# Attention followed by top-1 expert routing: earlier weight loads, shorter routing bookkeeping, and the left-over tile moved to the end

## The chip, the cores and the metric

The kernel runs on one core of a Trainium2 chip. A core has a matrix engine (TensorE, PE in the profile), a vector engine (VectorE, DVE), an engine for activations (ScalarE, ACT), a general engine (GpSimd, POOL), an engine that here only starts transfers (SyncE, SP) and 16 DMA engines that all transfers share. Each compute engine works through its own list of instructions in order and waits for the others at semaphores. The metric is the device time of one execution in microseconds (us). The kernel before was run three times: 325.83, 327.12 and 322.86 us, median 325.83. The profile is of a further execution of 325.04 us, whose span from the first to the last instruction is 323.0 us.

## The reference, cut to what matters

```python
kv  = einsum('bhsd,bhse->bhde', k, v)              # b=8, h=8, s=576, d=64
o   = einsum('bhsd,bhde->bhse', q, kv)             # attention without softmax
x   = o / sqrt(mean(o*o) + 1e-6) * g_norm          # per head; then 4608 rows x 512
logits = x @ w_gate                                # 8 experts
expert = argmax(logits);  gate = softmax(logits)[expert]
for e in range(8):                                 # w1: 512 x 1024, w2: 1024 x 512
    xe = x[expert == e]
    out[expert == e] = gate * (relu(xe @ w1[e]) @ w2[e])
```

Inputs and outputs are in 32-bit floats. Every row goes to exactly one expert; how many rows an expert gets is known only at run time.

## The kernel before, in words

**Attention stage (up to about 135 us).** The 4608 rows are treated in 36 *slots* of 128 rows. Four groups P of two batches each have nine slots: four for the first batch, four for the second, and one for the remaining 64 + 64 rows. For a batch, k-transposed-times-v is summed in PSUM (`kv_mm`), copied out, and extended with gate columns (`kv_gate`), so that the product with q gives the output rows and the logits at once. A slot s consists of `x_qt` (transposes of q, two slots ahead), `x_qs` (ScalarE copies them out), `x_mm` (the product, tile `op`), and `x_norm` with its inner `rest` (the norm: ScalarE squares `op` into `sq`, VectorE sums to `ms`, ScalarE makes `lnt` and `rinv`, VectorE writes `lr`, the scaled logits, and `xg`, the scaled rows in 16 bits).

Rows of `xg` are 516 sixteen-bit values wide: 512 of data, then the row's token number (512:514) and its gate weight (514:516).

**Routing.** Every four or five slots (a `Route`) the rows so far are sorted. `first` makes the one-hot choice `oh`; `ranks` counts, with matmuls of ones and of a triangular matrix, how many earlier rows chose the same expert (tile `pp`); `send` turns this into a row number `sli` in the DRAM scratch `xs_scratch`, which has 4608 places for each expert (`eoff` holds 4608 x e); `scatter` lets GpSimd start an indirect DMA of 128 rows to their places. A running count per expert (`csum`) carries over from group to group.

**Order.** All five engines' lists are written by hand: the loop over the 36 slots calls what the lists `mid[s]`, `late[s]` and `last[s]` hold, filled by `at(...)` (lines 440 to 487). `mid` runs before the slot's norm, `late` between `ms` and `lr`, `last` at the end of the slot. `pace` puts a tiny GpSimd copy ahead of each scatter, which reads `lr` of a named slot and so holds the scatter back until that slot. Loads of q, k and v (tag `ld`, six buffers of 8 KB per partition) and of expert weights are issued by SyncE in program order; each waits for its buffer to be free.

**Seam.** After slot 35 the last two tiles are routed (`tail`), the final counts become `cnt`, `valid`, `bigm` and the table of rows to gather, `rowi`. Expert 0's weights were loaded during slot 21's place in the order; ScalarE now casts them to 16 bits (`half1` also multiplies w1 by the norm's gain, `half2` casts w2). Expert 1's two loads are issued here, w1 when expert 0's w1 is cast, w2 when its w2 is cast, because one 32-bit staging buffer serves each. Then GpSimd gathers rows of experts 0 and 1 from `xs_scratch` (lines 609 and 719). A gather can start only when all scatters have landed. While it waits, TensorE runs `zeros` (matmuls of zeros that keep it busy, line 126).

**Expert stage.** Every expert has five tiles of 128 rows; rows beyond 640 of an expert go to left-over tiles. In this draw there is one. A `Job` has `flip(t)` (turn a tile: four transposes, a VectorE copy into `xt`, and the output row numbers `idx`), `one(ws, f)` (four matmuls of 320 columns, tile `hp`, then Relu on ScalarE into `ht`; sixteen of these), and `two(t)` (eight matmuls of 512 columns, tile `yp`, the gate weight on VectorE into `ys`, and a scatter to the output). In the loop over jobs (line 729) the next expert's weights are cast between the matmuls: `half1` on VectorE beside `one`, `half2` on ScalarE beside `two`, and as each staging buffer falls free the load of the expert after next is issued. The turns of the next expert's tiles stand among the last `one`s. The order of the jobs is experts 0 to 6, then the left-over tile, then expert 7. The left-over tile's expert number is read from a table at run time, so its loads are addressed by a register. If there were more left-over tiles, a loop after expert 7 (line 759) would take them.

The two pools of tiles, one for attention and one for the experts, use the same memory one after the other.

Of the kernel before, what the change touches and what calls it, by code (L numbers as in the profile page):

```python
# [11 lines left out]
F32 = mybir.dt.float32  # L12
F16 = mybir.dt.float16
# [15 lines left out]
def kernel(  # L29
# [11 lines left out]
    nc = tc.nc  # L41
# [41 lines left out]
    c_f32 = nc.inline_tensor(c32, name="c_f32")  # L83
    c16 = np.zeros((128, 384), np.float16)
    c16[:, 0:128] = np.eye(128)
    c16[:, 128:256] = ar[:, None] < ar[None, :]
    c16[:, 256:384] = 1.0
    c_f16 = nc.inline_tensor(c16, name="c_f16")

# [3 lines left out]
    cf = P_const.tile([128, c32.shape[1]], F32, tag="cf")  # L93
    ch = P_const.tile([128, 384], F16, tag="ch")
    ident = cf[:, 0:128]
# [7 lines left out]
    utri = ch[:, 128:256]  # L103
    ones = ch[:, 256:384]
    wg = P_const.tile([128, 4, 8], F32, tag="wg")
    g2 = P_const.tile([128, 1], F32, tag="g2")
    gw = P_const.tile([128, 4, 2, 8], F32, tag="gw")
    epsb = P_const.tile([128, 1], F32, tag="epsb")
    csum = P_const.tile([128, 8], F32, tag="csum")
    valid = P_const.tile([128, E, CT], F32, tag="valid")  # L110
# [18 lines left out]
    class Weights:  # L129
        def __init__(self, e):  # L130
            self.e = e if isinstance(e, bass.DynSlice) else slice(e, e + 1)

        def stage1(self):
            self.s1 = P_w.tile([128, 4, F], F32, tag="ws1", bufs=1, name="ws1")
            nc.sync.dma_start(
                self.s1, moe_w1[self.e, :, :].rearrange("o (t p) f -> p (o t) f", p=128)
            )

        def stage2(self):
            self.s2 = P_w.tile([128, 8, D], F32, tag="ws2", bufs=1, name="ws2")  # L140
            nc.sync.dma_start(
                self.s2, moe_w2[self.e, :, :].rearrange("o (t p) d -> p (o t) d", p=128)
            )

        def half1(self, eng, kk):
            if kk == 0:
                self.w1 = P_w.tile([128, 4, F], F16, tag="w1e", bufs=2, name="w1e")
            if eng is nc.scalar:
                eng.activation(self.w1[:, kk, :], self.s1[:, kk, :], ACTF.Copy, scale=g2)
            else:  # L150
                eng.tensor_scalar(  # L151
                    self.w1[:, kk, :], self.s1[:, kk, :], g2, 1.0,
                    op0=ALU.mult, op1=ALU.mult,
                )

        def half2(self, kk):
            if kk == 0:
                self.w2 = P_w.tile([128, 8, D], F16, tag="w2e", bufs=2, name="w2e")
            nc.scalar.copy(  # L159
                self.w2[:, 2 * kk:2 * kk + 2, :], self.s2[:, 2 * kk:2 * kk + 2, :]  # L160
            )

    ENG = mybir.EngineType
    by_hand = {ENG.PE, ENG.Activation, ENG.DVE, ENG.Pool, ENG.SP}
    order = list(range(E - 1)) + ["left", E - 1]
    W = [Weights(e) if e != "left" else None for e in order]

    with (
# [119 lines left out]
        qts, xgs, lrs = {}, {}, {}  # L288
        tail = None

        def x_qt(s):
# [32 lines left out]
        def x_norm(s, op):  # L324
            P, r, b = split(s)
            if r == 0:
                xgs[P] = PA.tile([128, 9, RW], F16, tag="xg", bufs=2, name="xg")
                lrs[P] = PA.tile([128, 9, 8, 8], F32, tag="lr", bufs=2, name="lr")
            xg, lr = xgs[P], lrs[P]
            oc = op[:, :, 0:288].rearrange("p c (i n) -> p c i n", n=144)  # L330
# [29 lines left out]
        class Route:  # L360
# [3 lines left out]
            def first(self):  # L364
# [19 lines left out]
                nc.vector.tensor_tensor(self.oh, cd, _bc(m2, 2, 8), op=ALU.is_equal)  # L384
                self.cs16 = PA.tile([128, 8], F16, tag="cs16", bufs=2, name="cs16")
                nc.vector.tensor_copy(self.cs16, csum)
                self.dl = dl

            def ranks(self):

                G, oh = self.G, self.oh
                self.pp = PSA.tile([128, G, 8], F32, tag="misc", bufs=1, name="pp")
                pp = self.pp
                nc.tensor.matmul(pp, ones, _bc(self.cs16, 1, G), start=True, stop=False)
                for t in range(G - 1):
                    nc.tensor.matmul(
                        pp[:, t + 1:G, :], ones, _bc(oh[:, t, :], 1, G - 1 - t),
                        start=False, stop=False,
                    )
                nc.tensor.matmul(pp, utri, oh, start=False, stop=True)  # L400
                ex = PA.tile([128, G, 8], F32, tag="ex", bufs=2, name="ex")
                nc.scalar.activation(ex, self.dl, ACTF.Exp)
                tsum = PA.tile([128, 8], F32, tag="tsum", bufs=2, name="tsum")
                nc.vector.reduce_sum(tsum, oh.transpose([0, 2, 1]), axis=AXX)
                nc.vector.tensor_add(csum, csum, tsum)
                se = PA.tile([128, G], F32, tag="se", bufs=2, name="se")
                nc.vector.reduce_sum(se, ex, axis=AXX)
                xg, g0 = xgs[self.P], self.g0
                nc.vector.reciprocal(
                    xg[:, g0:g0 + G, 514:516].bitcast(F32).rearrange("p g o -> p (g o)"), se  # L410
                )
                nc.vector.tensor_copy(
                    xg[:, g0:g0 + G, 512:514].bitcast(I32).rearrange("p g o -> p (g o)"),
                    tokc[:, 9 * self.P + g0:9 * self.P + g0 + G],
                )

            def send(self):
                G, g0 = self.G, self.g0
                t1 = PA.tile([128, G, 8], F32, tag="t1", bufs=2, name="t1")
                nc.vector.tensor_tensor(t1, self.pp, _bc(eoff, 1, G), op=ALU.add)  # L420
                t2 = PA.tile([128, G, 8], F32, tag="t2", bufs=2, name="t2")
                nc.vector.tensor_tensor(t2, t1, self.oh, op=ALU.mult)
                sl = PA.tile([128, G], F32, tag="sl", bufs=2, name="sl")
                nc.vector.reduce_sum(sl, t2, axis=AXX)
                sli = PA.tile([128, G], I32, tag="sli", bufs=4, name="sli")
                nc.vector.tensor_copy(sli, sl)
                self.sli = sli

# [46 lines left out]
        for P, g0, G in groups + [(3, 0, 4), (3, 4, 3)]:  # L475
            rt = Route(P, g0, G)
            s = 9 * P + g0 + G - 1
            at(last, s, rt.first)
            at(mid, s + 2, rt.ranks)
            at(late, s + 2, rt.send)  # L480
            s0 = s + 2 if P == 3 or (P, g0) == (2, 4) else s + 3
            for t in range(G):
                at(last, min(s0 + t, 35), pace, min(s0 + t, 35))
                at(last, min(s0 + t, 35), rt.scatter, t)

        at(last, 21, W[0].stage1)
        at(last, 21, W[0].stage2)


        load_first()  # L490
        nc.vector.memset(zero16, 0.0)
        nc.vector.memset(epsb, 1e-6)
        nc.vector.memset(csum, 0.0)
        nc.vector.memset(gw, 0.0)
# [45 lines left out]
        tail.ranks()  # L540
        cs16 = PA.tile([128, 8], F16, tag="cs16", bufs=2, name="cs16")
        nc.vector.tensor_copy(cs16, csum)
        tail.send()
        for t in range(2):
            tail.scatter(t)
        cp = PSA.tile([128, 8], F32, tag="misc", bufs=1, name="cp")
        nc.tensor.matmul(cp, ones, cs16, start=True, stop=True)
        nc.vector.tensor_copy(cnt, cp)
        nc.vector.tensor_tensor(valid, _bc(rankc, 1, E), _bc(cnt, 2, CT), op=ALU.is_lt)
# [4 lines left out]
        for kk in range(4):  # L554
            W[0].half1(nc.scalar, kk)
        W[1].stage1()
        for kk in range(4):
            W[0].half2(kk)
        W[1].stage2()


    with (
# [142 lines left out]
        with tc.manual_schedule(engines=by_hand):  # L705
# [17 lines left out]
            zp = PSF.tile([128, 512], F32, tag="yp", bufs=3, name="yp")  # L723
            zeros(zp, 8)
            for t in range(3):
                jobs[0].flip(t)
                zeros(zp, 2)

            for n in range(len(order)):
                job = jobs[n]  # L730
                if n == 3:
                    jobs[7] = left_over(0, 3 * CT, out_views[E * CT])
                    W[7] = jobs[7].w
                nxt = jobs[n + 1] if n + 1 < len(order) else None
                rows(n + 2)
                flips = list(range(nxt.nt)) if nxt is not None else []
                for ws in range(job.halves):
                    for f in range(8):
# [3 lines left out]
                        if ws == job.halves - 1 and f >= 2 and flips:  # L742
                            nxt.flip(flips.pop(0))
                        if ws == 0 and f % 2 == 1 and nxt is not None:
                            W[n + 1].half1(nc.vector, f // 2)
                            if f == 7 and n + 2 < len(order):
                                W[n + 2].stage1()
                for kk in range(max(job.nt, 4)):
                    if kk < job.nt:
                        job.two(kk)  # L750
                    if kk < 4 and nxt is not None:
                        W[n + 1].half2(kk)
                        if kk == 3 and n + 2 < len(order):
                            W[n + 2].stage2()
# [44 lines left out]
```

## Time and profile before

| What | Value | From |
|---|---|---|
| span of the profiled execution | 323.0 us | head of the page |
| TensorE busy | 275.5 us, 85% | page, part 1 |
| VectorE, ScalarE, GpSimd busy | 170.9, 158.1, 154.9 us | page, part 1 |
| bytes moved by DMA | 85.66 MB, mean 265 GB/s | page, part 2 |
| mean granted TensorE clock | 0.944 of full | the cores' view |
| last attention product starts (slot 35) | 129.65 us | timeline |
| first gather starts | 150.10 us | timeline |
| first expert matmul | 159.21 us | timeline |
| expert 1, start to end of its matmuls | 179.11 to 197.55 us | chain in order of time |
| left-over tile | 288.71 to 294.46 us | timeline |
| last expert's second products end | 317.74 us | timeline |

How to read it: the busy share of an engine is an average over three stages that are limited by different things, so it decides nothing by itself. One asks of each stage what the last wait before its end was. The timeline lists instructions by start; an entry such as `[3.95 <-ACT ht L663]` says that the engine stood idle for 3.95 us before it, and that the last thing to come was the ScalarE instruction of line 663 writing `ht`. A DMA instruction's row shows only its issue; its landing comes later. Numbers after an L are lines of the kernel before.

### The profile page before, as it was taken

How to read it: one execution, taken by the hardware profiler on the slowest of the kernel's cores; microseconds unless marked ns; L12 is line 12 of the kernel's file. 1: busy time of each engine (PE TensorE's matmuls, PEld its weight loads, DVE VectorE, ACT ScalarE, POOL GpSimd, SP SyncE). 2: the span in 40 equal slices, each digit the busy share in tenths (PEclk: the TensorE clock that was granted, in tenths of full speed). 3: DMA queues.
4: the chain of work that ended last, by engine and by line, in shares of the span. 5: the costliest groups of instructions: out<-in, count | busy, mean ns of one | idle time of the engine just before them, and what ended most of it. 6: DMA issues, size and time to landing. Idle time of an engine off the chain costs nothing.

```text
span 323.0 us, 6221 instructions
## 1 busy us (share of the span) xinstructions
PE 275.5 (85%) x2333; PEld 190.0 (59%) x2333; DVE 170.9 (53%) x467; ACT 158.1 (49%) x338; POOL 154.9 (48%) x208
## 2 busy tenths in 40 slices
PE   8787899999799976340799999999999999996893
PEld 3466788878687865210474655657475665654551
DVE  0042677787878778820266946455354546155022
ACT  1052455546456465380165573736466473834620
POOL 9322044448437654563773476467473315551014
PEclk9997999999999999565599999999999999999798
DMA  7999999999999950159457999979998978995004
GB/s 199 340 280 254 279 280 342 301 311 364 268 270 374 404 205 33 65 189 403 137 161 279 315 345 311 386 224 371 297 374 301 329 288 256 402 293 224 0 0 155
DMA packets 59759, 85.66 MB, mean 265 GB/s; under 512 B 16461, under 2 KB 41294, under 8 KB 59728
## 3 DMA queue, kind: packets, MB, share of 16 engines
q1 hardware_dynamic: 50480, 65.09, 63.9%
q0 software_dynamic: 6976, 18.96, 16.4%
q10 hardware_dynamic: 2272, 1.20, 1.4%
q8 instruction: 19, 0.31, 0.4%
q14 instruction: 12, 0.10, 0.1%
HBM read 71.70 MB, written 15.50 MB: 270 GB/s over the span
## 4 chain that ended last, share of the span: by engine, by line
PE 38%; DMA 11%; issue 4%; POOL 2%; DVE 1%; POOLq 1%
PE hp L656 18%; PE yp L670 16%; DMA out_dram<-ys,idx 10%; PE xp L637 3%; DMA xe<-xs_scratch,rowi 2%; POOL xs_scratch L430 1%; PE yp L126 1%; POOL out_dram L678 1%; DVE w1e L151 0%; POOLq L794 0%; POOL xe L609 0%; DVE xt L640 0%; POOLq L678 0%; POOLq L609 0%; DVE idx L642 0%
## 5 line engine op out<-in xcount | busy, mean ns | idle before, releaser
L663 ACT ACTIVATE ht<-hp 128x320 f16<-128x320 f32 (+1 forms) x136 | 57.7, 428 | 74.8 <-PE hp L656 50.1
L656 PE MATMUL hp<-xt,w1e 128*128 128x320 f16 (+1 forms) x544 | 81.6, 300 | 4.0 <-ACT ht L663 3.9
L678 POOL DMA_INDIRECT out_dram<-ys,idx x41 | 42.6, 1039 | 72.4 <-DVE ys L675 66.0
L670 PE MATMUL yp<-w2e,ht 128*128 128x512 f16 x328 | 72.3, 379 | 0.0
L656 PEld LDWEIGHTS <-w1e 128*128 128x128 f16 x544 | 51.6, 100 | 24.6 <-issue 4.7
L675 DVE TENSOR_SCALAR ys<-yp,xe 128x512 f32<-128x512 f32 x41 | 30.6, 750 | 58.0 <-PE yp L670 57.9
L670 PEld LDWEIGHTS <-ht 128*128 128x128 f16 x328 | 32.1, 98 | 37.1
L318 PE MATMUL op<-kvs,qts 128*128 128x144 f32 (+1 forms) x320 | 46.1, 307 | 8.5 <-DVE xg L353 4.1
L609 POOL DMA_INDIRECT xe<-xs_scratch,rowi x40 | 41.5, 1037 | 18.5 <-issue 14.3
L318 PEld LDWEIGHTS op<-kvs,qts 128*128 128x128 f32 (+1 forms) x320 | 38.4, 186 | 12.3 <-ACT sq L334 4.4
L430 POOL DMA_INDIRECT xs_scratch<-xg,sli x36 | 35.2, 978 | 12.9 <-issue 12.6
L640 DVE COPY xt<-xp 128x512 f16<-128x512 f16 x41 | 17.3, 423 | 39.9 <-PE xp L637 23.6
L159 ACT CAST w2e<-ws 128x1024 f16<-128x1024 f32 x36 | 34.8, 1042 | 2.7 <-DMA ws<-in_moe_w_dram 2.7
L236 POOL COPY qp<-ld 128x512 f32<-128x512 f32 x32 | 18.5, 615 | 31.8 <-DMA ld<-in_q_dram 31.8
L339 DVE TENSOR_REDUCE ms<-sq 128x8 f32<-128x512 f32 x36 | 24.4, 677 | 8.4 <-ACT sq L334 8.4
L637 PE MATMUL xp<-ch,xe 128*128 128x128 f16 x164 | 16.5, 226 | 13.5 <-DMA xe<-xs_scratch,rowi 12.7
L343 ACT ACTIVATE lnt<-ms,epsb 128x8 f32<-128x8 f32 x36 | 10.9, 302 | 34.3 <-DVE ms L339 34.3
L334 ACT ACTIVATE sq<-op 128x512 f32<-128x512 f32 x36 | 21.3, 590 | 10.9 <-PE op L318 10.6
L255 PE MATMUL kvp<-ld 128*64 128x64 f32 x512 | 21.9, 228 | 4.3 <-DMA ld<-in_v_dram 4.3
L353 DVE TENSOR_TENSOR xg<-op,rinv 128x512 f16<-128x512 f32 x36 | 24.5, 680 | 0.3 <-DMA xs_scratch<-xg,sli 0.3
L305 ACT COPY qts<-qtp 128x512 f32<-128x512 f32 x36 | 20.9, 581 | 6.5 <-PE qtp L300 6.4
L637 PEld LDWEIGHTS <-xe 128*128 128x128 f16 x164 | 12.9, 101 | 18.2 <-DMA xe<-xs_scratch,rowi 13.6
(92 smaller groups left out, 260.3 us busy)
## 6 DMA issues: line engine op xcount, KB each, us to landing
ws<-in_moe_w_dram SPq DMA_DIRECT2D x18, 2048.0 KB, 11.1
ld<-in_q_dram SPq DMA_DIRECT2D x8, 1024.0 KB, 10.7
ld<-in_k_dram SPq DMA_DIRECT2D x7, 1024.0 KB, 10.3
ld<-in_v_dram SPq DMA_DIRECT2D x7, 1024.0 KB, 10.6
kr<-in_k_dram SPq DMA_DIRECT2D x8, 128.0 KB, 9.9
ld<-in_k_dram SPq DMA_DIRECT2D x2, 512.0 KB, 7.3
ld<-in_v_dram ACTq DMA_DIRECT2D x2, 512.0 KB, 8.7
qr<-in_q_dram SPq DMA_DIRECT2D x8, 128.0 KB, 8.6
```

What stands on the lines that cost most here:

```text
L159: nc.scalar.copy(self.w2[:, 2 * kk:2 * kk + 2, :], self.s2[:, 2 * kk:2 * kk + 2, :])
L318: nc.tensor.matmul(op[c, i // 2, c0:c0 + 144], qts[s][:, i, c], kvs[:, i, :], start=True, stop=True,)
L339: nc.vector.reduce_sum(ms, sq, axis=AXX)
L353: nc.vector.tensor_tensor(xg[:, r, 0:512].rearrange("p (c i h n) -> p c i h n", c=2, i=2, h=2), ox, _bc(r4, 4, 64), op=ALU.mult,)
L430: nc.gpsimd.indirect_dma_start(out=xs_views[9 * self.P + self.g0 + t], out_offset=IndirectOffsetOnAxis(ap=self.sli[:, t:t + 1], axis=0), i ...
L609: nc.gpsimd.indirect_dma_start(out=xe.bitcast(I32), out_offset=None, in_=xs.ap(), in_offset=IndirectOffsetOnAxis(ap=rows, axis=0), bounds_ ...
L637: nc.tensor.transpose(xp[:, c, :], xe[t][:, c * 128:(c + 1) * 128], ident16)
L656: nc.tensor.matmul(hp, self.w.w1[:, kk, f * 128:(f + 1) * 128], self.xt[:, kk, ws * wd:(ws + 1) * wd], start=(kk == 0), stop=(kk == 3),)
L663: nc.scalar.activation(self.ht[:, f, ws * wd:(ws + 1) * wd], hp, ACTF.Relu)
L670: nc.tensor.matmul(yp, self.ht[:, f, t * 128:(t + 1) * 128], self.w.w2[:, f, :], start=(f == 0), stop=(f == 7),)
L675: nc.vector.tensor_scalar(ys, yp, self.xe[t][:, 514:516].bitcast(F32), None, op0=ALU.mult)
L678: nc.gpsimd.indirect_dma_start(out=self.views[t], out_offset=IndirectOffsetOnAxis(ap=self.idx[:, t:t + 1], axis=0), in_=ys, in_offset=None ...
```

## The change

It has six parts.

1. *Routing with fewer VectorE operations.* The running count starts from a constant that already holds each expert's offset (`base`, 36 x e in each of 128 partitions, so that the sum over partitions is 4608 x e). It is kept in 16 bits, a new tile for each group. So the copy of `csum` to 16 bits, the addition of `eoff` and the final cast of the index are no longer needed. The token numbers are written by GpSimd, once for nine slots. What `ranks` did on VectorE moves into `send`, behind the index.
2. *Scatters of the last group P = 3 without `pace`*, and two per slot.
3. *Expert 1's weights are loaded during attention*, into four buffers of the tag `ld` that q, k and v no longer use (`stage_in`), and are cast at the seam: w1 on VectorE, w2 on ScalarE in eight pieces of 512 columns.
4. *Expert 2's loads are issued early but held*: two one-element memsets on VectorE, behind the first three turns of expert 0, stand ahead of them.
5. *24 instead of 8 matmuls of zeros* at the seam.
6. *The left-over tile comes after expert 7.* The casts of the next expert's weights begin with job 1, as experts 0 and 1 have theirs.

```diff
-    c16 = np.zeros((128, 384), np.float16)
+    c16 = np.zeros((128, 392), np.float16)
...
+    c16[:, 384:392] = (N // 128) * np.arange(8)
...
+    base = ch[:, 384:392]
...
-        def stage1(self):
+        def stage1(self, hold=False):
             self.s1 = P_w.tile([128, 4, F], F32, tag="ws1", bufs=1, name="ws1")
+            if hold:
+                nc.vector.memset(self.s1[:, 0, 0:1], 0.0)
             nc.sync.dma_start(
...
+        def stage_in(self, pool, tag, bufs):
+
+            self.s1, self.s2 = [], []
+            for dst, src in ((self.s1, moe_w1), (self.s2, moe_w2)):
+                rows = src[self.e, :, :].rearrange("o (t p) f -> p (o t) f", p=128)
+                n = rows.shape[1] // 2
+                for m in range(2):
+                    t = pool.tile([128, n, rows.shape[2]], F32, tag=tag, bufs=bufs, name="ws")
+                    nc.sync.dma_start(t, rows[:, n * m:n * m + n, :])
+                    dst.extend([t[:, kk, :] for kk in range(n)])
...
+            if isinstance(self.s2, list):
+                for m in (2 * kk, 2 * kk + 1):
+                    nc.scalar.copy(self.w2[:, m, :], self.s2[m])
...
-    order = list(range(E - 1)) + ["left", E - 1]
+    order = list(range(E)) + ["left"]
...
+                nc.gpsimd.tensor_copy(
+                    xgs[P][:, :, 512:514].bitcast(I32).rearrange("p g o -> p (g o)"),
+                    tokc[:, 9 * P:9 * P + 9],
+                )
...
-                self.cs16 = PA.tile([128, 8], F16, tag="cs16", bufs=2, name="cs16")
-                nc.vector.tensor_copy(self.cs16, csum)
...
-                nc.tensor.matmul(pp, ones, _bc(self.cs16, 1, G), start=True, stop=False)
+                nc.tensor.matmul(pp, ones, _bc(csum[-1], 1, G), start=True, stop=False)
...
-                nc.vector.tensor_tensor(t1, self.pp, _bc(eoff, 1, G), op=ALU.add)
-                t2 = PA.tile([128, G, 8], F32, tag="t2", bufs=2, name="t2")
-                nc.vector.tensor_tensor(t2, t1, self.oh, op=ALU.mult)
...
+                nc.vector.tensor_tensor(t2, self.pp, oh, op=ALU.mult)
+                self.sli = PA.tile([128, G], I32, tag="sli", bufs=4, name="sli")
+                with nc.allow_low_precision("sums of whole numbers"):
+                    nc.vector.reduce_sum(self.sli, t2, axis=AXX)
...
+                with nc.allow_low_precision("sums of whole numbers below 2048"):
+                    nc.vector.reduce_sum(tsum, oh.transpose([0, 2, 1]), axis=AXX)
+                    nc.vector.tensor_add(cs, csum[-1], tsum)
+                csum.append(cs)
...
-                at(last, min(s0 + t, 35), pace, min(s0 + t, 35))
-                at(last, min(s0 + t, 35), rt.scatter, t)
+                if P < 3:
+                    at(last, s0 + t, pace, s0 + t)
+                at(last, min(s0 + t // (2 if P == 3 else 1), 35), rt.scatter, t)
 
         at(last, 21, W[0].stage1)
         at(last, 21, W[0].stage2)
+        at(last, 30, W[1].stage_in, PA, "ld", 6)
...
             W[0].half1(nc.scalar, kk)
-        W[1].stage1()
         for kk in range(4):
             W[0].half2(kk)
-        W[1].stage2()
+        for kk in range(4):
+            W[1].half1(nc.vector, kk)
+        for kk in range(4):
+            W[1].half2(kk)
...
-            zeros(zp, 8)
+            zeros(zp, 24)
             for t in range(3):
                 jobs[0].flip(t)
                 zeros(zp, 2)
 
+            W[2].stage1(hold=True)
+            W[2].stage2(hold=True)
...
-                if n == 3:
-                    jobs[7] = left_over(0, 3 * CT, out_views[E * CT])
-                    W[7] = jobs[7].w
+                if n == 4:
+                    jobs[E] = left_over(0, 3 * CT, out_views[E * CT])
+                    W[E] = jobs[E].w
...
-                        if ws == 0 and f % 2 == 1 and nxt is not None:
+                        if n > 0 and ws == 0 and f % 2 == 1 and nxt is not None:
...
-                    if kk < 4 and nxt is not None:
+                    if n > 0 and kk < 4 and nxt is not None:
```

## The prediction

> **What bounds the kernel now.** I read the busy slices of the page first. They put the lost time in two places.
>
> ```profile
> PE   8787899999799976340799999999999999996893
> ...
> PEclk9997999999999999565599999999999999999798
> DMA  7999999999999950159457999979998978995004
> ```
>
> Each digit is a slice of 8.07 us. TensorE drops from slice 14 to 19 (113 to 161 us), where the DMA engines stand nearly empty for two slices (15 and 16, up to 137 us) and then fill again. It drops once more near the end. The chain that ended last, in order of time, shows what the seam between attention and experts waits for:
>
> ```profile
> 142.48 0.96 POOL xs_scratch L430
> 143.44 5.68 issue
> ...
> 150.10 5.25 DMA xe<-xs_scratch,rowi
> ...
> 159.42 2.72 PE hp L656 x16
> ...
> 162.95 1.50 DVE w1e L151 x2
> ```
>
> The last scatter of rows starts at 142.48; the gathers, which must wait for all scatters, start only at 150.10 and the first lands 5.25 us later. The table by stretches says why both transfers are slow:
>
> ```profile
> 130.00:140.00 10.00, 3.36 (x27) 2.10 (x24) 8.24 (x42) 5.60 (x11) 6.04 (x12) 0.50 0.19 67
> 140.00:150.00 10.00, 2.70 (x7) 0.69 (x5) 0.00 (x0) 4.16 (x5) 2.84 (x3) 0.67 0.88 316
> 150.00:155.00 5.00, 0.00 (x0) 0.00 (x0) 0.00 (x0) 0.00 (x0) 3.98 (x4) 0.50 1.05 383
> ```
>
> The last three columns are clock, DMA share, GB/s. Expert 1's 4.2 MB go out at 140.41 and 144.19, just when scatters and gathers need the engines. The issue table for 121 to 140 us gives 2.5 us from issue to landing for a scatter with the engines free; over the whole run the median is 6.1.
>
> The timeline of the end shows the second loss:
>
> ```profile
> 295.94 3.88 ACT L159 CAST w2e<-ws 128x1024 f16<-128x1024 f32 x4 [2.72 <-DMA ws<-in_moe_w_dram]
> ...
> 300.21 8.90 PE L656 MATMUL hp<-xt,w1e 128*128 128x320 f16 x52 [3.95 <-ACT ht L663]
> ...
> 308.94 8.80 PE L670 MATMUL yp<-w2e,ht 128*128 128x512 f16 x40
> ...
> 318.94 0.98 POOL L678 DMA_INDIRECT out_dram<-ys,idx  x1 [0.71 <-DVE ys L675]
> ```
>
> The left-over tile (288.71 to 294.46) is too short to hide expert 7's weights. Their casts start late, expert 7's Relus queue behind them on ScalarE, and TensorE waits. Expert 7 takes 23.28 us (to 317.74) against 18.44 for experts 1 to 5, each evenly. In between TensorE is the bound: 18 of 18 us busy.
>
> In attention VectorE sets the pace. The timeline of one slot with routing:
>
> ```profile
> 124.66 0.19 DVE L404 TENSOR_REDUCE tsum<-oh 128x8 f32<-128x32 f16 x1
> ...
> 125.33 0.68 DVE L339 TENSOR_REDUCE ms<-sq 128x8 f32<-128x512 f32 x1
> ...
> 126.59 0.17 DVE L426 CAST sli<-sl 128x4 int32<-128x4 f32 x1
> ...
> 126.67 0.21 DVE L347 TENSOR_TENSOR lr<-op,rinv 128x64 f32<-128x64 f32 x1
> ```
>
> Five counting operations stand ahead of ms, four behind it, and lr comes only after these.
>
> **What the Trainium skill says.** "ScalarE: Activation LUTs", What ACT_TABLE_LOAD costs: an activation without pointer operands takes 186 ns + 0.833 ns per column, and neighbours overlap by 93 ns. The trace agrees: 1042 ns for the 1024-column cast (1039 by the formula), 0.97 us apart. "SBUF — State Buffer", Who interferes with whom: a VectorE tensor_scalar may hold the port that GpSimd needs for its descriptors. The trace fits: gathers beside a w1e cast took 1.40 and 1.48 us, others 1.00. "TensorE: Matmul & The Clock Gate", Part 1: after an idle window of some 3.4 us the clock is halved until about as long a busy one. Here the clock is 0.50 from 150 to 160 us, and expert 0's first 16 matmuls took 2.93 us against 2.15 (16 x 0.1346) later.
>
> **The change, part by part.**
>
> *Leaner counting.* Each group loses four VectorE operations (copy of csum, eoff add, index cast, token copy, the last one to GpSimd, once per nine slots, where it lies beside waiting). The rest moves behind ms. The slot above went 124.66 to 126.67, 2.01 us. After: ms 0.59, then six operations, three dependent ones at 0.22 and three at 0.09, 0.94: together 1.53. Saved 0.48, with the csum copy 0.55. From 47 us on no engine is seen waiting for an attention load except q's, and seven groups follow: 3.9 us at most. The last three, whose loads had landed, give 1.6 at least. q of batch 5 landed at about 80.2 and was used at 80.70, so part is held by loads: I take 2.8.
>
> *Expert 1's load.* On SyncE it stands after expert 0's load, so behind all attention loads. Pieces 1 and 3 wait for buffers free by 103 us, piece 4 for the last k matmul of batch 7 (113). 4.2 MB at the 380 GB/s of 105 to 115 us is 11 us, into slices that were empty: landed by about 130, before its casts. Cost nothing.
>
> *Scatters.* The last nine go out at 129.01, 130.34, 133.28, 135.96 (slots 27 to 30, each held by the tick for the slot named in the plan), then every 1.3 from 137.29 to 142.48. Without the ticks the first four follow each other and end by 133.8, so the next three start when their index is ready (134.5 on the old clock), the last two 1.27 apart behind them: 139.6 instead of 142.48. The four new w1e casts on VectorE fall beside them (0.5 back): 2.4 gained. With 2.8: start at 137.3. Landing after 2.5, not 6.6: 139.8. First gather 1.0 later as before (149.12 to 150.10): 140.8. Third gather 2.7 later, landed 2.6 to 2.9 after that: 146.3.
>
> *A new wait.* In the built order the first turn of expert 0 (the copy into xt) waits for the last cast of expert 1's w2, because its pool reuses that memory; behind it on VectorE stand the other turns, idx and the two memsets that release expert 2's load; TensorE's third turn waits for a transpose buffer, its first hp for xt, and ScalarE's Relus for hp. VectorE's own four casts of expert 1's w1 stand ahead of it and need pieces 1 and 2, long landed. ScalarE starts casting at 136.14 - 2.8 = 133.3, does expert 0's eight in 8.0 (136.14 to 144.16), then eight of 512 columns, 0.52 each by the price above (qts, 0.58 alone, is the nearest row): 4.2. So 145.6. Then three turns of which two are transposed already: 1.7. Both paths meet; first expert matmul at 147.3 instead of 159.2. The 24 zero matmuls (8 before, 0.45 each cold) end near 144 and cost nothing, but should leave the clock warm.
>
> *Expert 0.* It loses its w1e casts (on the chain for 1.50) and the cold start: 18.44 + two own turns at 0.22 + 0.2 = 19.1. But expert 2's load, held to about 147, now meets the gathers for expert 1. The fifth of these starts at 140.8 + 9 x 1.32 = 152.7, lands 6 later, 158.7; its turn is due at about 157.1. Bounds 0 (landing as when free) and 3: I take 1.6. Together 20.7. The two memsets of one column are hidden by the wait for gathers.
>
> *Left-over last.* Experts 1 to 6: 6 x 18.44 = 110.6. Expert 7 with one turn: 17.4, as expert 6 before (271.32 to 288.71), its weights fetched at the normal distance. Left-over: 32 matmuls at 0.07, a Relu 0.35, eight at 0.216: 4.3. Its weights and casts have all of expert 7 to hide in. The end as before: 317.74 to 323.0, 5.3.
>
> Sum: 147.3 + 20.7 + 110.6 + 17.4 + 4.3 + 5.3 = 305.6, against 323.0: 17.4 less, of which the tail is about 6. From the median 325.83: 308.4.
>
> **The rivals.** *A: the new waits eat part of the seam.* Attention gains only 1, so ScalarE ends at 147.4; scatters are held longer by the port, and expert 1's last gather is 3 late. Then start 149.2, expert 0 22.1: 3.3 more, 311.7; with cold matmuls and piece 4 late by 2, up to 315. For it: ScalarE and gather paths come within 1 us of each other, so either slipping shows. *B: the tail gain fails.* DMA is 0.93 busy in steady experts; if the left-over's weights, addressed by a register, come as late as expert 7's did, 5 to 6 return: 314. Against: expert 2 to 6 never show that wait at the same distance. *C: slower.* DMA is saturated from 40 to 115 us; if 4.2 MB at 333 GB/s, 12.6 us, fell in front of attention's loads and nothing else but the tail came through (5.4), 325.8 + 12.6 - 5.4 = 333. Against: SyncE's order.
>
> **How the numbers follow.** Main case 0.72 (304 to 311), A 0.14, B 0.10, C 0.04. The predicted time is the main case's, 308.4. The range reaches from 303.5 (attention's full 3.9, no gather stall: 308.4 - 1.1 - 1.6 = 305.7, and two less for the spread of 4 in the times before) to 315, the upper end of A and past B. Within 2% means above 319.3: only much of A and B together, 0.05. Slower by over 2%: C, 0.03. Faster 0.92.
>
> **What would show it.** DMA slices 15 and 16 full; a scatter landing in 2.5 us at the end of attention; the first xt copy ended by ScalarE's w2e cast near 145.6; hp at 147 with a clock of 1.0; a wait for a gather at the end of expert 0; experts at 18.44; no ScalarE wait in expert 7; about 4.3 us of left-over matmuls. It would be wrong if VectorE's casts held GpSimd for their whole 3 us, if attention were held by its loads, or if expert 2's late load let the experts' weights fall behind.

## The result, and the profile after

The changed kernel takes 307.25 us in the median (305.59 to 308.73, four runs); the kernel before took 324.35 beside it (322.77 to 327.12, four runs). The ratio is 0.946, with a 95% interval from 0.936 to 0.956. The profiled executions have spans of 303.6 and 323.0 us. The prediction was 308.4.

The busy slices of the changed kernel, each 7.59 us long:

```profile
PE   8697989899989987647979999999999999999993
...
PEclk9799999999999999869999999999999999999998
DMA  6999999999999999922894299979799898968421
```

TensorE's hole has shrunk from six slices to four (15 to 18, 114 to 144 us), none of them empty, and the dip near the end is gone. Part of this is no work: the 24 matmuls of zeros fill 7.57 us there, where the 8 of the kernel before filled 3.60. The DMA engines are full up to slice 16, at two tenths in 17 and 18, and nearly full again in 19 and 20, where expert 2's load runs: the quiet time now lies where scatters and gathers need it. The table by stretches (columns as before: clock, DMA share and GB/s at the end) shows the same:

```profile
130.00:140.00 10.00, 7.11 (x24) 2.83 (x25) 6.04 (x22) 9.07 (x11) 6.06 (x6) 0.66 0.21 76
140.00:150.00 10.00, 8.29 (x63) 4.81 (x61) 2.46 (x11) 6.28 (x14) 7.72 (x8) 1.00 0.58 171
150.00:155.00 5.00, 4.55 (x38) 2.69 (x36) 1.65 (x7) 2.62 (x6) 3.78 (x5) 1.00 1.00 363
```

Before, 140 to 150 us had 316 GB/s of expert weights and 2.70 us of TensorE, all of it zeros; now it has 171 GB/s and 8.29 us, of which 2.81 are zeros. The timeline of the seam, in the changed kernel's line numbers (450 scatter, 630 gather, 658 transposes of a turn, 661 copy into `xt`, 137 and 145 the memsets, 677 first products):

```profile
135.17 1.07 POOL L450 DMA_INDIRECT xs_scratch<-xg,sli  x1 [0.30 <-issue]
138.80 1.04 POOL L630 DMA_INDIRECT xe<-xs_scratch,rowi  x1 [2.56 <-issue]
138.99 4.25 ACT L177 CAST w2e<-ws 128x512 f16<-128x512 f32 x8
...
141.46 1.00 POOL L630 DMA_INDIRECT xe<-xs_scratch,rowi  x1 [0.30 <-issue]
...
143.32 0.42 DVE L661 COPY xt<-xp 128x512 f16<-128x512 f16 x1 [6.59 <-PE xp L658]
...
144.26 0.40 PE L658 MATMUL xp<-ch,xe 128*128 128x128 f16 x4 [0.52 <-DVE xt L661]
...
145.20 0.06 DVE L137 MEMSET ws<- 128x1 f32 x1
...
145.22 2.33 PE L677 MATMUL hp<-xt,w1e 128*128 128x320 f16 x16
```

The first gather follows the last scatter by 3.6 us, not 7.6. The first `xt` copy starts 0.08 us after ScalarE's last cast (138.99 + 4.25 = 143.24), although the row names transposes, of which this turn's own ended at 141.99. The third turn, on which the first products wait, comes at 144.26: the row names the first copy, which ended half a microsecond before; its gather had gone out 2.8 us earlier, the time that a gather takes to land here. The held loads leave at 145.35 and 146.30. What they do next stands in the chain:

```profile
135.17 1.07 POOL xs_scratch L450
136.24 1.58 issue
...
150.57 6.77 DMA xe<-xs_scratch,rowi
157.34 0.05 issue
157.39 0.40 PE xp L658 x4
...
158.33 8.63 PE yp L691 x40
```

A gather for expert 1, issued beside the 4.2 MB of expert 2, lands after 6.77 us and holds up the last turn of expert 1's tiles, which stands among expert 0's last products.

The end, where TensorE now waits for no weights:

```profile
286.91 3.87 ACT L179 CAST w2e<-ws 128x1024 f16<-128x1024 f32 x4
...
295.01 2.11 PE L677 MATMUL hp<-xt,w1e 128*128 128x128 f16 x32
...
296.96 1.89 PE L691 MATMUL yp<-w2e,ht 128*128 128x512 f16 x8
...
299.91 0.98 POOL L699 DMA_INDIRECT out_dram<-ys,idx  x1 [2.51 <-DVEq L783]
```

### The profile page after: what moved, and what is told of

Same layout as the page of the kernel before. It is cut to its first block, busy times and chain, and to the rows that moved or that the text cites. A ratio compares the mean times of both kernels' runs of the same rounds, so it can differ in the third digit from the quotient of the medians.

```text
span 303.6 us, 6229 instructions
## 1 busy us (share of the span) xinstructions
PE 275.5 (91%) x2349; PEld 189.7 (62%) x2349; DVE 164.0 (54%) x431; ACT 159.2 (52%) x342; POOL 153.2 (50%) x205
## 4 chain that ended last, share of the span: by engine, by line
PE 30%; issue 10%; DMA 9%; POOL 4%; POOLq 1%
PE yp L691 14%; PE hp L677 14%; DMA out_dram<-ys,idx 7%; POOL out_dram L699 2%; DMA xe<-xs_scratch,rowi 2%; PE xp L658 2%; POOL xe L630 2%; POOLq L818 0%; POOL xs_scratch L450 0%; POOLq L699 0%; POOLq L630 0%; POOLq L783 0%
## 5 line engine op out<-in xcount | busy, mean ns | idle before, releaser
L677 PE MATMUL hp<-xt,w1e 128*128 128x320 f16 (+1 forms) x544 | 79.3, 294 | 0.1
L677 PEld LDWEIGHTS <-w1e 128*128 128x128 f16 x544 | 50.3, 98 | 18.8 <-issue 0.6
L630 POOL DMA_INDIRECT xe<-xs_scratch,rowi x40 | 40.5, 1012 | 14.4 <-issue 10.2
L661 DVE COPY xt<-xp 128x512 f16<-128x512 f16 x41 | 17.4, 425 | 37.2 <-PE xp L658 37.2
L179 ACT CAST w2e<-ws 128x1024 f16<-128x1024 f32 x32 | 31.0, 1042 | 0.0
L326 ACT COPY qts<-qtp 128x512 f32<-128x512 f32 x36 | 20.9, 582 | 7.8 <-PE qtp L321 7.8
L275 PEld LDWEIGHTS kvp<-ld 128*64 128x64 f32 x512 | 17.7, 137 | 8.5 <-issue 7.5
L168 DVE TENSOR_SCALAR w1e<-ws,g 128x1024 f16<-128x1024 f32 x32 | 22.2, 756 | 0.0
```

The costliest lines, as they stand in the source:

```text
L179: nc.scalar.copy(self.w2[:, 2 * kk:2 * kk + 2, :], self.s2[:, 2 * kk:2 * kk + 2, :])
L275: nc.tensor.matmul(kvp[64 * hh:64 * hh + 64, i, :], lhs, rhs, start=(j == 0), stop=(j == 4),)
L630: nc.gpsimd.indirect_dma_start(out=xe.bitcast(I32), out_offset=None, in_=xs.ap(), in_offset=IndirectOffsetOnAxis(ap=rows, axis=0), bounds_ ...
L677: nc.tensor.matmul(hp, self.w.w1[:, kk, f * 128:(f + 1) * 128], self.xt[:, kk, ws * wd:(ws + 1) * wd], start=(kk == 0), stop=(kk == 3),)
```

## The experiments

Attention ends at times that differ by 2 to 3 us between executions of equal attention code. So each kernel is cut at three points of its trace: A is the start of slot 35's last norm (`lr`), "seam" runs from A to the first expert product, "expert 0" from there to its last product, "rest" to the end of the span. Expert 0's end is where the chain's second products end.

| Kernel (same kind of chip) | A | seam | expert 0 | rest | span |
|---|---|---|---|---|---|
| before | 134.94 | 24.27 | 19.9 | 143.9 | 323.0 |
| tail_alone_2 | 132.09 | 24.00 | 19.2 | 136.6 | 311.9 |
| no_hold | 129.93 | 23.97 | 19.2 | 136.6 | 309.7 |
| late_w1_2 | 131.08 | 22.46 | 19.9 | 136.7 | 310.1 |
| paced | 131.01 | 18.74 | 21.1 | 137.1 | 307.9 |
| after | 129.85 | 15.37 | 21.8 | 136.6 | 303.6 |
| after_again | 129.28 | 15.56 | 20.9 | 136.6 | 302.3 |
| zeros8 | 129.06 | 15.77 | 20.8 | 136.6 | 302.2 |
| hold_longer_2 | 131.30 | 15.57 | 19.2 | 136.6 | 302.7 |
| best1 | 130.49 | 15.82 | 19.2 | 136.6 | 302.1 |

The first four experiments ran on another chip, where the kernel before itself took 350.84 us; there only ratios to that and the seam are read.

### The job order alone

The kernel before, with one edit, run on both chips:

```diff
-    order = list(range(E - 1)) + ["left", E - 1]
+    order = list(range(E)) + ["left"]
...
-                if n == 3:
+                if n == 4:
```

> The kernel before, with only the order of the jobs changed: left-over tile after expert 7. Theory (the left-over tile was too short to hide expert 7's weights): in the profile of before the stretch from expert 6's first matmul to the end took 51.7 us (271.32 to 323.0), in the changed kernel the same jobs took 44.4 (259.1 to 303.6). So 7.2 us less than before, about 317, and no wait of ScalarE for weights in the last expert. Rival (the tail gain needs the earlier loads at the seam as well): less than 2 us, ScalarE still waits for a load near the end.

On the slower chip: 341.88 us, ratio 0.972 (0.964 to 0.981), seam 24.35.

> The kernel before with one edit, the left-over tile's job behind expert 7. My theory: all of its gain lies behind expert 6, where the two profiles differ by 7.2 us; so 6.5 to 7.5 us less than the kernel before (about 317.5), the seam unchanged (first expert product 24 to 25 us after slot 35's last norm), no wait of TensorE for ScalarE in expert 7, and an end after expert 7's products of 4 + 4.8 us. Rival: part of the 7.2 belongs to the weights that the changed kernel loads early; then 3 to 5 us less and a wait for weights stays in the last expert.

On a chip like the first: 314.82 us against 323.07, ratio 0.975 (0.965 to 0.985). The seam is as before, and the rest is 136.6 us, to 0.1 us that of the changed kernel. The end of its timeline (lines 159 the cast, 656 and 670 the products, 678 the scatter):

```profile
295.26 3.87 ACT L159 CAST w2e<-ws 128x1024 f16<-128x1024 f32 x4
...
303.36 2.11 PE L656 MATMUL hp<-xt,w1e 128*128 128x128 f16 x32
...
305.31 1.89 PE L670 MATMUL yp<-w2e,ht 128*128 128x512 f16 x8
...
308.26 0.98 POOL L678 DMA_INDIRECT out_dram<-ys,idx  x1 [2.52 <-DVE ys L675]
```

The seam is untouched, and the job order by itself gives the whole gain of the tail, 143.9 - 136.6 = 7.3 us; the rival, that early weights had a part in it, is out. The 8.2 us between the medians agrees within the interval.

### Routing alone, and expert 1's load at the seam

The first is the kernel before with the shorter counting and unpaced scatters (parts 1 and 2 of the change), on the slower chip.

> The kernel before, with only the shorter counting and the untimed scatters of the last group; loads, job order and zeros as before. Theory (VectorE's chain paces attention): the last slot's logits come 5 us earlier, as in the changed kernel (129.85 against 134.94), the last scatter starts about 7 earlier, but the landing of the last scatter and the first gather stay slow (6 and 5 us beside expert 1's load): total 6 to 7 us less than before, about 318. Rival (attention gained because expert 1's load changed what the queues do): under 2 us less.

It took 342.2 us, ratio 0.975 (0.968 to 0.982). I had expected slot 35's logits 5 us earlier; against tail_alone, which has the old counting on the same chip, they are 2.2 us earlier (134.38 against 136.54). Its last scatter starts 5.15 us behind A (before: 7.54), but the first gather still follows 7.73 us later, and the first copy into `xt` 7.0 us after that. Of the 2.4 us only 1.2 reach the first product (seam 23.10).

The second is the changed kernel with expert 1's loads, and the casts that follow them, where the kernel before has them, and no hold:

```diff
-        at(last, 30, W[1].stage_in, PA, "ld", 6)
...
+        W[1].stage1()
         for kk in range(4):
             W[0].half2(kk)
+        W[1].stage2()
```

> The changed kernel, but expert 1's weights are loaded at the seam and cast beside expert 0, as before, and expert 2's are not held. Theory (the seam was slow because this load shared the DMA engines with scatters and gathers): last scatter lands in 6 instead of 2.7 us, first gather in 5 instead of 2.7, so the first expert matmul 5 to 6 us later; expert 0 loses its waits for gathers (2.6) but has the casts on VectorE again; together 4 to 6 us slower than the changed kernel, 312 to 313. Rival (the shift came from routing alone): within 1 us of the changed kernel.

On the slower chip: 337.3 us, ratio 0.963 (0.956 to 0.971), seam 22.50.

> The changed kernel with expert 1's two loads at the seam as in the kernel before, without the hold. My theory: the load falls on the last scatters and on the gathers as it did before; the first gather starts 7.5 us after the last scatter instead of 3.6, the first expert product 22 to 23 us after slot 35's last norm instead of 15.4, and expert 0 takes 18.6 to 19.5 instead of 20.9 to 21.8: in sum 4 to 6 us slower than the changed kernel, about 310 to 312. Rival: the early load costs attention what it gives at the seam; then slot 35 ends 2 us or more earlier here than in the changed kernel and the time is within 2 us of it.

On a chip like the first: 311.79 us (310.99 to 312.84), ratio 0.963 (0.956 to 0.970). Its timeline at the seam (627 gather, 655 transposes):

```profile
136.23 0.96 POOL L450 DMA_INDIRECT xs_scratch<-xg,sli  x1 [0.30 <-issue]
...
143.73 1.03 POOL L627 DMA_INDIRECT xe<-xs_scratch,rowi  x1 [6.54 <-issue]
...
149.73 0.61 PE L655 MATMUL xp<-ch,xe 128*128 128x128 f16 x4 [8.14 <-DMA xe<-xs_scratch,rowi]
```

7.5 us from scatter to gather and 6.0 to its landing: about as before the change (7.6 and 5.3). The early load and the hold together are worth 22.46 - 15.4 = 7.0 us of seam, less 1 to 2 in expert 0. A at 131.08 lies in the range of the seven kernels that load expert 1 early (129.06 to 131.30), so the early load costs attention nothing that can be seen; the rival, which needs 2 us or more, finds no support. A smaller cost isn't excluded by single traces: on the slower chip the kernel that loads early (hold_longer) has A at 135.94, the two without at 134.23 and 134.38.

### The hold

The changed kernel without the two memsets, so that expert 2's loads leave when expert 0's weights are cast:

```diff
-            W[2].stage1(hold=True)
-            W[2].stage2(hold=True)
+            W[2].stage1()
+            W[2].stage2()
```

> The changed kernel without the two memsets: expert 2's loads go out as soon as expert 0's casts free the buffers, 135 and 139 us. Theory (loads at the seam slow scatters and gathers): the last scatter lands in about 5 instead of 2.7 us, the first three gathers in 5 to 6, first expert matmul 4 to 6 us later; in return expert 0 without waits for gathers (2.6 less); in all 2 to 3 us slower. Rival (the hold only moves the same cost into expert 0): same as the changed kernel within 1 us.

312.88 us, ratio 0.969 (0.961 to 0.978). The changed kernel, run again beside it:

> The changed kernel once more, as the yardstick of the runs beside it: if the chip is like that of the first result, 305 to 309; on a slower chip the same ratio to before, 0.946, is expected by the theory that nothing in the gain depends on the chip; a ratio nearer to 1 would say that the gathers, waits or instruction starts that grew on the slower chip eat the gain.

305.18 us, ratio 0.943 (0.936 to 0.950). The timeline of the kernel without the hold:

```profile
135.24 1.07 POOL L450 DMA_INDIRECT xs_scratch<-xg,sli  x1 [0.30 <-issue]
...
143.29 1.04 POOL L630 DMA_INDIRECT xe<-xs_scratch,rowi  x1 [6.98 <-issue]
...
150.08 0.61 PE L658 MATMUL xp<-ch,xe 128*128 128x128 f16 x4 [9.59 <-DMA xe<-xs_scratch,rowi]
```

The loads left at 135.40 and 139.17. The tables of transfers give the number of transfers and the median us from issue to landing: first for the kernel without the hold (scatters, then gathers), then scatters of the changed kernel beside it and gathers of the changed kernel's first profile.

```profile
xs_scratch<-xg,sli POOLq DMA_INDIRECT x4, 7.0
xe<-xs_scratch,rowi POOLq DMA_INDIRECT x6, 5.6
...
xs_scratch<-xg,sli POOLq DMA_INDIRECT x4, 2.9
...
xe<-xs_scratch,rowi POOLq DMA_INDIRECT x8, 2.9
```

Behind A the first gather starts 4.4 us later than in the changed kernel beside it, because the scatters land later, and its own landing takes 3.9 us more. I had expected the first product 4 to 6 us later and a loss of 2 to 3; it comes 8.4 us later behind A; expert 0 gets 1.7 us back, and 7.7 us are lost between the medians. The direction was right, the size was not: a load in this place is paid for twice, once by the scatters and once by the gathers. Without the hold the seam is 23.97 us, no better than before the change: loading expert 1 early is worth nothing by itself, if expert 2's load then takes its place.

### A longer hold

Expert 2's loads are issued in job 0 when all turns of expert 1 are done, some 11 us later behind A than in the changed kernel:

```diff
-            W[2].stage1(hold=True)
-            W[2].stage2(hold=True)
...
+                            if n == 0 and not flips:
+                                W[2].stage1(hold=True)
+                                W[2].stage2(hold=True)
```

> The changed kernel, with expert 2's two loads held until the last turn of expert 1's tiles instead of the third turn of expert 0's. Theory (expert 0 took 21.75 us because the gathers of expert 1's tiles land in 6 us beside that load): gathers land in 2.7, TensorE waits for none, expert 0 takes 19.1 to 19.4, total 2.4 less than the changed kernel, about 305. Rival 1 (the turns wait because GpSimd starts a gather only every 1.3 us): no change. Rival 2 (expert 2's weights then come late): expert 1 or 2 longer than 18.44, total the same or more.

On the slower chip: 334.65 us, ratio 0.955 (0.948 to 0.961), the lowest median of the four there; seam 15.58.

> The changed kernel with expert 2's loads held until the last turn of expert 1's tiles, again, beside the changed kernel on the same chip. Theory (expert 0 is long because the gathers of expert 1's tiles land in 6 us beside expert 2's load): expert 0 19.1 to 19.4 instead of 21.75 us, 2.4 less in all. Rival 1 (gathers start too far apart): no change. Rival 2 (expert 2's weights late): expert 1 longer than 18.44.

On a chip like the first: 303.87 us, ratio 0.938 (0.932 to 0.943), beside 305.18 for the changed kernel. The waits between 150 and 170 us in the changed kernel run beside it (us in total, times, longest):

```profile
PEld L658 <- DMA xe<-xs_scratch,rowi: 1.6, 3, 0.8
...
PE xp L658 <- DMA xe<-xs_scratch,rowi: 0.4, 1, 0.4
```

In the kernel with the longer hold that stretch shows no wait of TensorE for a gather, and its DMA engines are at a quarter of their time (150 to 155 us):

```profile
150.00:155.00 5.00, 5.00 (x45) 3.59 (x44) 1.49 (x7) 3.50 (x8) 3.78 (x5) 1.00 0.25 71
```

Expert 0 takes 19.2 us, as expected, and later experts are not late (rest 136.6). The stage is 1.7 to 2.6 us shorter; the medians differ by 1.3. Of the 1.7 us against the kernel beside it, 0.5 is not the hold's: there the first 16 products ran at a lower clock and took 2.86 us against 2.33 (clock 0.75 and 1.00 from 140 to 145 us). The intervals of the two ratios overlap, so it is the profile's stage that tells them apart. This one and the last below have the lowest medians of all versions.

### Fewer zero matmuls

```diff
-            zeros(zp, 24)
+            zeros(zp, 8)
```

> The changed kernel with 8 zero matmuls at the seam instead of 24. Theory (24 keep the clock at full for the first expert matmuls): clock near 0.5 when the gathers land, turns and the first 16 hp matmuls longer, 0.6 to 1.5 us slower. Rival (the wait for ScalarE and the gathers hides it): no change.

304.8 us, ratio 0.942 (0.935 to 0.948): no difference to 305.18. The clock was 0.50 from 140 to 145 us against 0.75, but the first product starts at 144.83 against 144.84, since other waits end there; the first 16 products took 2.78 us against 2.86. The theory that 24 zeros keep the clock full for the first products failed, and the rival holds.

### Paced scatters in the last group

```diff
-                if P < 3:
-                    at(last, s0 + t, pace, s0 + t)
-                at(last, min(s0 + t // (2 if P == 3 else 1), 35), rt.scatter, t)
+                at(last, min(s0 + t, 35), pace, min(s0 + t, 35))
+                at(last, min(s0 + t, 35), rt.scatter, t)
```

> The changed kernel with the ticks ahead of the scatters, one scatter in a slot, kept in the last group too. My theory: after slot 35's last norm the last scatter starts 7.4 us later instead of 5.3, gathers and the first expert product follow it by the same 2 us unless ScalarE's casts, which end within 1 us of the third gather, hid part; so 1.0 to 2.2 us slower than the changed kernel. Rival: the casts on ScalarE set the start alone; then the last scatter comes 2 us later and the first expert product at the same distance of 15.4 us from slot 35's last norm, and the time is the same.

308.87 us, ratio 0.952 (0.943 to 0.960). The last scatter starts 8.27 us behind A, not 7.4: the later scatters fall beside VectorE's casts, where one took 1.30 us. Gather and first product follow with the whole 3 us, so ScalarE hid nothing; expert 0's first 16 products, cold (clock 0.50 from 145 to 150 us), took 3.35 us. Seam and expert 0 are 2.7 to 3.4 us longer than in the changed kernel. The mechanism was right and its size too small by 1 us; the rival is out.

### Half of ScalarE's casts on VectorE

The longer hold and, for expert 1's w2:

```diff
-                for m in (2 * kk, 2 * kk + 1):
-                    nc.scalar.copy(self.w2[:, m, :], self.s2[m])
+                nc.scalar.copy(self.w2[:, 2 * kk, :], self.s2[2 * kk])
+                nc.vector.tensor_copy(self.w2[:, 2 * kk + 1, :], self.s2[2 * kk + 1])
```

> The changed kernel with expert 2's loads held until expert 1's last turn, and of expert 1's w2 casts every second one on VectorE instead of ScalarE. ScalarE's casts behind expert 0's eight then take some 2.1 us instead of 4.25. My theory: the start of expert 0 is set by two things that come within 1 us of each other, ScalarE's casts and the third gather's landing; taking half of one away gives at most 0.3 us beside the longer hold alone (303.9), the first copy into xt now ends a wait for a gather or follows VectorE's own casts, and the first expert product starts 14.8 to 15.5 us after slot 35's last norm, as before. Rival: ScalarE alone set it, then the first expert product comes 1.0 to 1.5 us earlier and the time is about 302.6. Second rival: the four casts on VectorE hold GpSimd's gathers, and it is 0.5 to 1 us slower.

303.65 us, ratio 0.938 (0.930 to 0.946): as with the longer hold alone (0.938). The timeline:

```profile
139.62 2.17 ACT L176 CAST w2e<-ws 128x512 f16<-128x512 f32 x4
...
142.31 1.00 POOL L630 DMA_INDIRECT xe<-xs_scratch,rowi  x1 [0.30 <-issue]
...
143.08 0.42 DVE L661 COPY xt<-xp 128x512 f16<-128x512 f16 x1 [4.37 <-PE xp L658]
...
145.35 0.40 PE L658 MATMUL xp<-ch,xe 128*128 128x128 f16 x4 [0.77 <-DMA xe<-xs_scratch,rowi]
...
146.31 2.34 PE L677 MATMUL hp<-xt,w1e 128*128 128x320 f16 x16
```

ScalarE is done at 141.79 and the first copy comes 0.9 us earlier behind A than with the longer hold alone, but the third turn still waits for the third gather, 3.0 us after that went out. The first product gains nothing (seam 15.82). Halving ScalarE's share brings no time: both waits ended together, and the gather's alone is enough to set the start.

## Why the prediction was right, step by step

The mechanism held in all parts but the warm clock, and the sum came out 1.2 us too high: 308.4 against 307.25. In spans it was 305.6 against 303.6.

*Counting and the end of attention.* Predicted 2.8 us earlier; the two profiles differ by 5.1 (134.94 to 129.85), more than my upper bound of 3.9. The slot with routing behind `ms`, in the changed kernel (364 is `ms`, 430 and 433 the index, 372 `lr`):

```profile
120.18 0.68 DVE L364 TENSOR_REDUCE ms<-sq 128x8 f32<-128x512 f32 x1
120.77 0.18 DVE L430 TENSOR_TENSOR t<-pp,oh 128x32 f32<-128x32 f32 x1
...
121.60 0.17 DVE L446 TENSOR_TENSOR cs<-cs,tsum 128x8 f16<-128x8 f16 x1
121.68 0.22 DVE L372 TENSOR_TENSOR lr<-op,rinv 128x64 f32<-128x64 f32 x1
```

From `ms` to `lr` it takes 1.50 us; I had worked out 1.53 for a stretch that took 2.01. From slot 31's `lr` to slot 32's the old counting takes 2.75 us and the new 2.24, from 34's to 35's 2.68 and 2.20, and without the copy of `csum` the slot before each is 0.06 to 0.07 shorter: 0.57 and 0.55 per group, where I had 0.55. So the surplus isn't the counting. Executions of equal attention code differ by 3.0 us already at slot 2 (its `lr` starts at 31.64 in zeros8 and at 34.61 in hold_longer_2), before any routing; that the landing of q, k and v makes this difference is likely but not shown. Of the later slots: tail_alone_2, with the old counting, has A at 132.09, and the eight with the new one average 130.25. Against the mean of the two old ones, 133.5, the gain is 3.3 us; counted from slot 2's `lr` it is 3.0; on the slower chip it is 1.7 (136.54 against a mean of 134.85). 2.8 is inside that, and some 2 us of the difference between the two profiles is chance. With two traces of the old counting per kind of chip at most, more can't be said.

*Expert 1's load at no cost.* late_w1_2 shows none of 2 us or more; a smaller one stays open.

*Scatters.* 2.2 us earlier behind A, predicted 2.4. Beside VectorE's casts they took 1.13 and 1.07 us instead of 0.96, 0.3 in all, where I gave 0.5. On the shared port that the prediction names, the Trainium skill, "SBUF — State Buffer", Who interferes with whom, says that whoever comes first keeps it for the whole instruction. Here one cast takes 0.75 us, and four of them cost two scatters 0.28 us in all; when a scatter needs the port is not to be seen, so this neither confirms nor refutes the page.

*Landings.* Predicted 2.5 us for scatters and 2.6 to 2.9 for gathers with free engines; measured 2.7 and 2.7 to 2.9, and 5 to 7 beside a weight load. The Trainium skill, "DMA: Bandwidth & Descriptors", Anatomy of one DMA, gives a fixed 2.0 us plus bytes at 436 GB/s; for a gather's 132 KB (128 rows of 1032 bytes) an estimate of 2.3. The trace of free engines is 0.4 to 0.6 above it; the page's fit has no term for the load beside it, which here is the larger part.

*The new wait.* Predicted: ScalarE's casts 4.2 us long and then three turns, first product 15.2 us behind A. Measured: 4.25 (the price in the Trainium skill, "ScalarE: Activation LUTs", What ACT_TABLE_LOAD costs, gives an estimate of 7 x 0.52 + 0.61 = 4.25) and 15.4 to 15.6. That both waits end together was foreseen; best1 and paced show that the gather's side is binding. (The 1024-column casts that the prediction has 0.97 us apart start 0.94 apart; 0.97 is 3.87 us divided by 4. The sum doesn't rest on it.)

*Zeros at no cost.* They cost nothing, but the second half of the sentence, that they should leave the clock warm, failed: in after_again the clock was 0.75 from 140 to 145 us with the same 24 zeros. It was also without worth, as zeros8 is as fast.

*Expert 0.* Predicted 20.7 with 1.6 us of waiting for gathers; measured 21.8 and 20.9, and 19.2 with that wait removed by the longer hold (predicted 19.1). The excess was 2.6 us in the first profile, all of it in the half with expert 1's turns; in after_again it was 1.7, of which 0.5 was the cold start that I had taken to be gone. I had priced the last turn alone; in the first profile TensorE stands at the last three of the five turns (0.35 us at 154.24, 0.78 at 155.96, 0.49 at 157.39), and its weight loads at all five.

*Left-over last.* Predicted 6.3 for the tail, measured 7.3. Experts 1 to 6 take 18.44 and expert 7 17.4, as forecast. The left-over products take 3.85 instead of 4.3 and the end 4.75 instead of 5.3: the second products start 1.95 us after the first, without the 0.35 us of Relu that I had put between them.

In sum: 5.1 instead of 2.8 for attention, 8.9 instead of 9.1 at the seam, 1.9 instead of 0.8 lost in expert 0, 7.3 instead of 6.3 at the end. That makes 19.4 us between the two profiles, where I had 17.4 and the medians have 17.1. The changed kernel's profile is of the fastest of its four executions (305.59), 1.7 us below their median, so the parts read from it are flattered. That the median came so close to the forecast is in part luck: the four parts were off by 2.3, 0.2, 1.1 and 1.0 us, not all the same way.

## What to carry to other kernels

Where small indirect transfers lie on the critical path, ask what else is on the DMA engines in those microseconds: moving one 4 MB load away gained nothing until the next one was held back too. A load that is hidden anyway should be held until the last of those transfers has landed; held a few microseconds too short, it gives part of the gain back. And put the piece of work that is too short to hide the next one's weights at the end, where nothing comes after it.

## What the runs showed of the hardware that was not expected

A second chip was 8% slower with the same kernel before (350.84 against 324.35 us). In late_w1 there, between 160 and 260 us, TensorE and VectorE stood for some microseconds at a time on "issue" and on each other (us in total, times, longest):

```profile
PEld L655 <- issue: 9.6, 7, 3.6
PE xp L655 <- DVE xt L658: 7.7, 6, 3.4
DVE xt L658 <- remote: 7.6, 2, 3.9
```

What delays them was not found; the seams there are as on the other chips (24.35 against 24.27 and 24.00; 22.50 against 22.46; 15.58 against 15.57). The ratio to the kernel before held for two kernels (0.972 and 0.975 for the job order, 0.963 and 0.963 for expert 1's load at the seam), but not for the longer hold: 0.955 there and 0.938 on the other chip, with intervals that lie apart. Its seam was as short there, but its expert 0 took 30.9 us instead of 19.2. So a gain at the seam can be eaten behind it, and a ratio found on one chip doesn't simply carry over to another.
